# Gathering an expert's rows two turns ahead in a fused attention and mixture-of-experts kernel

## The chip, the cores and the metric

One Trainium2 chip, one of its cores. The metric is the device time of one launch in microseconds, lower is better; the number compared is the median of several runs. TensorE is written PE (its weight loads PEld), VectorE DVE, ScalarE ACT, GpSimd POOL, SyncE SP.

## What is computed

A linear attention block without a mask, then a mixture of experts in which each token goes to one expert or to none. Everything is float32. Cut to what matters:

```python
# q, k, v: (8, 8, 576, 64);  w1: (8, 512, 1024);  w2: (8, 1024, 512)
kv  = einsum('bhsd,bhse->bhde', k, v)
o   = einsum('bhsd,bhde->bhse', q, kv)
o   = o / sqrt(mean(o * o, -1) + 1e-6) * g_norm
x   = o.transpose(0, 2, 1, 3).reshape(4608, 512)       # one row for each token
do  = x @ w_skip > 0                                   # the others keep x
e   = argmax(x @ w_gate, axis=1); gate = softmax(x @ w_gate)[e]
out = x.copy()
for each expert i:                                     # over rows with do and e == i
    out[rows] = x[rows] + gate[rows] * (relu(x[rows] @ w1[i]) @ w2[i])
```

## The kernel before

The first third of the kernel is the attention. Its result x is written to the output tensor in HBM (`out_dram` in the profile), and from there on the output tensor is also the place from which the experts read their rows. While the last x is made, tokens are counted for each expert, experts are put in order of their token counts (largest first), and each token gets a slot number; the tables `src` (row to read for a slot) and `rows` (row to write) follow from that.

Then come eight turns, r = 0 to 7, one expert each (`experts`, L1276). Turn r holds between 256 and 352 slots, cut into pieces: two of 128 rows and, in turns 0 to 5, one or two smaller ones (64 or 32 rows, whose tables are `asrc` and `arows`). For each turn these steps are made:

- **Gather.** `gather_all` (L1269) takes a buffer `xg` from a pool that has three of them in rotation (`bufs=3`, L1271; turn 0 has a buffer of its own, `xg0`) and issues one indirect DMA from POOL for each piece (`gather_piece`, L1000 in the profile), which reads rows of `out_dram`.
- **Transpose.** `expert_in` (L1004, transposes at L1010, copies at L1013 and L1015) turns each piece on PE by a product with the identity and lets ACT copy it from PSUM into `xt`.
- **Layer 1.** `fast_1` (L1126) multiplies w1 and `xt` in a seven-product (Strassen) scheme; the products are in `product` (L1113), the sums they need are on DVE (L1055, L1061, L1117) and the copies on ACT (L1123). The relu writes `ht` (L1175, L1179). Turn 0 uses the plain `layer_1` (L1034).
- **Layer 2.** `fast_2` (L1186) does the same with `ht` and w2 for the first two pieces; the smaller ones are done plainly (`layer_2`, L1045).
- **Result.** `result` (L1246) multiplies by the gate, adds x in place in `xg` on DVE (L1252), and POOL issues an indirect DMA that scatters the rows to `out_dram` (L1255).

The order of instructions on each engine is the program's order: the block from L138 to L1395 is scheduled by hand, and a framework adds the waits. Three of its waits matter here, and all stand in the instruction lists:

- A gather reads `out_dram`, so it waits until all scatters issued before it have landed, and a scatter waits until all gathers issued before it have landed. Scatters do not wait for each other (L1259).
- `xg` of turn r + 3 is the buffer of `xg` of turn r, so a gather into it also waits for the transposes and the scatters of the earlier tenant.
- POOL's own queue is in order: gathers, scatters and the `blank` memset of the unused columns of `ht` (L1028) run one after another, and an instruction that waits holds those behind it.

In turn r the transposes are those of the **next** turn, r + 1: the first piece's are put into the end of `fast_1` (`between`, ahead of the last w1 product), the others directly after it (L1305, L1306), so that PE has `xt` for the next turn while layer 2 runs. Weights are loaded by SP (`load_weights`, L319 and L324), two turns' sets alternating between two pools.

Of the kernel before, what the change touches and what calls it, by code (L numbers as in the profile page):

```python
# [17 lines left out]
def kernel(  # L18
# [204 lines left out]
    for a in range(2):  # L223
        r = slice(a * 64, (a + 1) * 64)
# [679 lines left out]
    with tc.tile_pool(name="wpool_b", bufs=1, reuse_waits="tile") as wpool_b, \  # L904
# [92 lines left out]
        def gather_piece(xg, piece, src, asrc):  # L997
            off, m, col = piece
            idx = src if m == P else asrc
            nc.gpsimd.indirect_dma_start(  # L1000
                out=x_of(xg, off, m), out_offset=None, in_=cut_rows(m)[:, :],
                in_offset=bass.IndirectOffsetOnAxis(ap=idx[:, col:col + 1], axis=0))

        def expert_in(xg, xt, piece):  # L1004
            off, m, _ = piece
            x = x_of(xg, off, m)
            n = DC * m // P
            xp = bank()[:, :].rearrange("p (j t) -> p j t", t=P)
            for j in range(n):
                last = nc.tensor.transpose(out=xp[:, j, :], in_=x[:, j * P:(j + 1) * P],  # L1010
                                           identity=ident[:, :])
            if m == P:
                nc.scalar.copy(out=xt[:, :, off:off + P], in_=xp[:, :, :])  # L1013
            else:
                nc.scalar.copy(  # L1015
                    out=xt[:, :, off:off + m].rearrange("p (q j) t -> p q j t", j=n),
                    in_=xp[:, 0:n, :].rearrange("p j (q t) -> p q j t", t=m))
            return last

        def new_xt():  # L1020
            return ffn.tile([P, DC, CAP], FP32, tag="xt", name="xt")
# [8 lines left out]
        def layer_1(r, xt, ht, cols, fs):  # L1030
            for f in fs:
                hps = bank()
                for dc in range(DC):
                    nc.tensor.matmul(out=hps[:, cols], lhsT=w_sb[r][0][:, dc, f * P:(f + 1) * P],  # L1034
                                     rhs=xt[:, dc, cols], start=(dc == 0), stop=(dc == DC - 1))
                nc.scalar.activation(out=ht[:, f, cols], in_=hps[:, cols], func=ACT.Relu)
# [32 lines left out]
        def w1_sums(r):  # L1069
            w1 = w_sb[r][0]  # L1070
            s = wsum_pool.tile([P, 3, HD, F // 2], FP32, tag="s1", name="s1")
            sums[r, "w1"] = s
            lo, hi = slice(0, F // 2), slice(F // 2, F)
            parts = [combine((s[:, 0, d, :], s[:, 1, d, :], w1[:, d, hi], s[:, 2, d, :]),
                             w1[:, d, lo], w1[:, HD + d, lo], w1[:, d, hi], w1[:, HD + d, hi])
                     for d in range(HD)]
            return [job for both in zip(*parts) for job in both]
# [13 lines left out]
        def x_sums(r, xt, n):  # L1091
            t = ffn.tile([P, 3, HD, CAP // 2], FP32, tag="xs", name="xs", bufs=1)
            sums[r, "x"] = t
            lo, hi, a, b = slice(0, n), slice(n, 2 * n), slice(0, HD), slice(HD, DC)
            return list(combine_moving((t[:, 0, :, lo], t[:, 1, :, lo], xt[:, a, hi], t[:, 2, :, lo]),
                                       xt[:, a, lo], xt[:, a, hi], xt[:, b, lo], xt[:, b, hi]))
# [8 lines left out]
        def do(work, n=None):  # L1105
            n = len(work) if n is None else min(n, len(work))
            for job in work[:n]:
                job()
            del work[:n]
# [136 lines left out]
        def result(piece, yps, xg, tables, group):  # L1246

            off, m, col = piece
            n = DM * m // P
            rows, gate = tables[0 if m == P else 1]  # L1250
            x = x_of(xg, off, m)
            nc.vector.scalar_tensor_tensor(  # L1252
                out=x, in0=yps[:, 0:n], scalar=gate[:, col:col + 1], in1=x,
                op0=ALU.mult, op1=ALU.add)
            ins = nc.gpsimd.indirect_dma_start(  # L1255
                out=cut_rows(m)[:, :],
                out_offset=bass.IndirectOffsetOnAxis(ap=rows[:, col:col + 1], axis=0),
                in_=x, in_offset=None, bounds_check=N * P // m - 1, oob_is_err=False)
            tc.declare_no_dep(ins.ins, group=group, reason="each row has one slot")  # L1259
            tc.add_to_no_dep_group(group, ins.ins)  # L1260

        def load_ahead(r, behind=None):
            for ahead in (r, r + 1):
                if ahead < E and ahead not in w_sb:
                    load_weights(ahead, wpool_b if ahead % 2 else wpool_a, behind)
# [3 lines left out]
        def gather_all(r, pieces, src, asrc):  # L1269
            if r < E:  # L1270
                xgs[r] = xg0 if r == 0 else gather_pool.tile([P, CK, DM], FP32, tag="xg", name="xg",  # L1271
                                                             bufs=3)
                for piece in pieces[r]:
                    gather_piece(xgs[r], piece, src, asrc)

        def experts(pieces, widths, srcs, xt, ht, yps0, tables, group):  # L1276

            for r in range(E):
                load_ahead(r)
                if yps0 is not None and r == E - 1:  # L1280
                    nc.gpsimd.drain()
                if r:
                    gather_all(r + 1, pieces, *srcs)
                todo = pieces[r]
                end = widths[r]
                new = {}

                def enter(some):
                    for piece in some:
                        expert_in(xgs[r + 1], new["xt"], piece)  # L1290

                more = pieces[r + 1] if r + 1 < E else []
                if more:
                    new["xt"] = new_xt()
                beside = []
                if r == 0:
                    if yps0 is not None:
                        tables = first_tables(lambda fs: layer_1(r, xt, ht, slice(P, end), fs), tables)
                        result((0, P, 0), yps0, xgs[0], tables, group)
                    else:  # L1300
                        layer_1(r, xt, ht, slice(0, end), range(FC))
                    do(w1_sums(r + 1))
                    enter(more)
                else:
                    fast_1(r, xt, ht, end // 2, w2_sums(r), lambda: enter(more[0:1]))  # L1305
                    enter(more[1:])  # L1306
                if more:
                    n = widths[r + 1] // 2
                    beside = x_sums(r + 1, new["xt"], n) + (w1_sums(r + 1) if r else [])
                if r == 0:  # L1310
                    for piece in todo:
                        result(piece, layer_2(r, ht, piece), xgs[r], tables, group)
                        do(beside, 4)
                    do(beside)
                else:
                    if yps0 is not None and r == 1:
                        rnd_i = rounds()
                    if yps0 is not None and r == E - 1:
                        n_rounds.append(nc.values_load(rnd_i[0:1, 0:1], min_val=1,
                                                       max_val=ROUNDS + 1))  # L1320
                    of = {piece[0:2]: piece for piece in todo}
                    fast_2(r, ht, todo[2:], beside,
                           lambda key, y: result(of[key], y, xgs[r], tables, group))
                del w_sb[r]
                if more:
                    xt, ht = new["xt"], new_ht()
                    if yps0 is not None:
                        blank(ht, r + 1)
# [52 lines left out]
        def first_tables(layer, tables):  # L1381

            gp = g_ps[:, GB:GB + 3 * NCOL]
            half = NT // 2
            for i, t in enumerate((0, half)):
                bv = columns(t, half, colid_i, gate_k, 3, slot_pool, half)
                layer(range(i * FC // 2, (i + 1) * FC // 2))
                place(gp, bv, t, half, t == 0, t == half)
            gate = slot_gates_of(gp)
            agate = slot_pool.tile([P, NRES], FP32, tag="agate", name="agate")  # L1390
            nc.vector.tensor_copy(out=agate[:, :], in_=again_of(gate))
            return (tables[0], gate), (tables[1], agate)
# [56 lines left out]
```

## Time and profile before

| | |
|---|---|
| median of 3 runs | 396.01 us (393.86, 396.01, 396.41) |
| profiled execution, device time | 393.16 us |
| its span, first to last instruction | 391.4 us |
| PE busy, weight loads busy | 363.3 us (93%), 314.0 us (80%) |
| DVE, ACT, POOL busy | 242.8, 143.4, 124.1 us |
| mean granted TensorE clock | 0.984 |
| DMA | 81.70 MB, 209 GB/s over the span |
| layer 1 of turn 1 begins on PE | at 170.2 us of the span |
| last product on PE ends, then last result and scatter | 382.8 us, 391.4 us |

All times inside the profile are microseconds from the start of the span of the one profiled execution. The device time is 1.8 us more than the span. "Busy" is the time in which an engine executed something; the idle time in brackets after a row of the timeline is the gap on that engine directly before the row, with what ended it. Products on PE overlap each other in its pipeline and their ends are modelled. A row with x4 or x8 joins that many instructions. A DMA row on POOL is the time in which POOL makes the descriptors; the transfer itself lands later, and "landing" is the time from the issue until the data are there.

### The profile page before, as it was taken

The numbers are of one execution on the slowest core, as the hardware profiler recorded it, in microseconds if no ns is written. First come the engines' busy times: TensorE is split into PE (matmuls) and PEld (weight loads), VectorE is DVE, ScalarE is ACT, GpSimd is POOL, SyncE is SP. The second block draws the span as 40 slices with busy tenths as digits, with TensorE's granted clock in tenths as the row PEclk, the third lists the DMA queues.
The fourth block names the chain that finished last, engine by engine and source line by source line (L and its number), as shares of the span: only waits on it lengthen the run. The fifth ranks groups of instructions, "written<-read, shape, count | busy, mean of one in ns | idle before, by whom it ended". The sixth has DMA issues, their size and how long they took to land.

```text
span 391.4 us, 9585 instructions
## 1 busy us (share of the span) xinstructions
PE 363.3 (93%) x3822; PEld 314.0 (80%) x3822; DVE 242.8 (62%) x615; ACT 143.4 (37%) x384; POOL 124.1 (32%) x194
## 2 busy tenths in 40 slices
PE   7779999999987989999999999999999999989991
PEld 4668798898876668589879979989989878979980
DVE  3244458667778752765846657767667757858711
ACT  2445676666773212124303512512411421421410
POOL 7024557655677360123013303303303203202002
PEclk8999999999999999999999999999999999999997
DMA  8999999985597269654607355565564563511001
GB/s 298 394 392 391 402 399 403 399 261 182 161 381 241 55 202 358 234 175 151 216 15 272 77 201 163 180 216 154 178 216 145 171 229 102 198 27 56 2 2 51
DMA packets 31672, 81.70 MB, mean 209 GB/s; under 512 B 2106, under 2 KB 2114, under 8 KB 31620
## 3 DMA queue, kind: packets, MB, share of 16 engines
q1 hardware_dynamic: 27824, 69.47, 50.8%
q0 software_dynamic: 3776, 11.53, 8.7%
q8 instruction: 32, 0.52, 0.6%
q14 instruction: 20, 0.16, 0.1%
q10 hardware_dynamic: 20, 0.02, 0.0%
HBM read 66.80 MB, written 14.48 MB: 208 GB/s over the span
## 4 chain that ended last, share of the span: by engine, by line
PE 66%; issue 12%; DMA 9%; POOL 5%; DVE 3%; ACT 2%; SPq 1%; POOLq 0%; DVEq 0%; ACTq 0%
PE bank L1113 33%; PE bank L1045 7%; PE o_ps L471 7%; DMA out_dram<-xg,rows 4%; PE sum_ps L355 4%; PE q_ps L435 4%; PE bank L1034 3%; PE g_ps L369 3%; DMA q<-in_q_dram 2%; POOL xb L542 2%; DMA xg<-out_dram,src 2%; PE bank L1010 2%; POOL out_dram L1255 1%; PE g_ps L387 1%; DMA xg<-out_dram,asrc 1%
## 5 line engine op out<-in xcount | busy, mean ns | idle before, releaser
L1123 ACT COPY p<-bank 128x128 f32<-128x128 f32 (+6 forms) x70 | 20.8, 297 | 105.3 <-PE bank L1113 91.2
L1113 PE MATMUL bank<-xt,w 128*128 128x128 f32 (+5 forms) x336 | 55.4, 288 | 0.0
L542 POOL TENSOR_TENSOR xb<-xl,g_b 128x512 f32<-128x512 f32 x36 | 43.7, 1216 | 35.5 <-DVE rs L507 33.7
L1113 PEld LDWEIGHTS bank<-xt,w 128*128 128x128 f32 x336 | 47.0, 190 | 1.9 <-DVE bank L1117 1.4
L1117 DVE TENSOR_TENSOR bank<-bank,p 128x128 f32<-128x128 f32 (+6 forms) x70 | 23.6, 337 | 39.7 <-PE bank L1113 38.9
L1255 POOL DMA_INDIRECT out_dram<-xg,rows x16 | 16.2, 1012 | 75.6 <-DVE xg L1252 74.1
L471 PE MATMUL o_ps<-kvd,qT 128*128 128x146 f32 x240 | 37.0, 296 | 1.8 <-ACT kvd L391 0.7
L1113 PE MATMUL bank<-xs,s 128*128 128x128 f32 (+5 forms) x224 | 36.7, 289 | 0.0
L1045 PE MATMUL bank<-w,ht 128*32 128x128 f32 (+2 forms) x448 | 36.6, 322 | 0.0
L493 DVE TENSOR_REDUCE rs<-sq 128x8 f32<-128x512 f32 x36 | 24.5, 682 | 17.2 <-ACT sq L485 17.1
L471 PEld LDWEIGHTS o_ps<-kvd,qT 128*128 128x128 f32 x240 | 32.5, 193 | 3.3 <-ACT kvd L391 1.5
L1255 POOL DMA_INDIRECT out_dram<-xg,arows x8 | 9.0, 1127 | 76.6 <-DVE xg L1252 76.3
L1000 POOL DMA_INDIRECT xg<-out_dram,src x15 | 16.8, 1123 | 49.8 <-DMA out_dram<-xg,rows 27.4
L1113 PEld LDWEIGHTS bank<-xs,s 128*128 128x128 f32 x224 | 31.1, 190 | 1.0 <-ACT p L1123 0.8
L1045 PEld LDWEIGHTS bank<-w,ht 128*32 128x32 f32 (+2 forms) x448 | 20.4, 121 | 13.6 <-issue 10.9
L355 PE MATMUL sum_ps<-v,k 64*64 64x64 f32 x1152 | 26.0, 231 | 2.4 <-issue 2.2
L512 DVE TENSOR_TENSOR xl<-o_ps,rs 128x584 f32<-128x584 f32 x33 | 25.3, 766 | 4.3 <-PE o_ps L471 0.5
L1113 PE MATMUL bank<-w,ht 128*128 128x256 f32 x112 | 27.2, 386 | 0.0
L1113 PE MATMUL bank<-t,ht 128*128 128x256 f32 x112 | 27.1, 385 | 0.0
L355 PEld LDWEIGHTS sum_ps<-v,k 64*64 64x64 f32 x1152 | 22.2, 142 | 6.1 <-issue 3.8
L1113 PE MATMUL bank<-t,hs 128*128 128x256 f32 x112 | 25.3, 379 | 0.0
L485 ACT ACTIVATE sq<-o_ps 128x512 f32<-128x512 f32 x33 | 19.7, 597 | 15.2 <-PE o_ps L471 14.5
(203 smaller groups left out, 665.2 us busy)
## 6 DMA issues: line engine op xcount, KB each, us to landing
w<-in_moe_w_dram SPq DMA_DIRECT2D x16, 2048.0 KB, 8.7
q<-in_q_dram SPq DMA_DIRECT2D x8, 1152.0 KB, 9.0
k<-in_k_dram SPq DMA_DIRECT2D x7, 1152.0 KB, 12.1
v<-in_v_dram SPq DMA_DIRECT2D x7, 1152.0 KB, 15.2
out_dram<-xb SPq DMA_DIRECT2D x29, 256.0 KB, 9.0
out_dram<-xb POOLq DMA_DIRECT2D x7, 256.0 KB, 6.6
k<-in_k_dram SPq DMA_DIRECT2D x2, 576.0 KB, 5.2
v<-in_v_dram SPq DMA_DIRECT2D x2, 576.0 KB, 6.2
```

Source lines behind the costliest of these rows:

```text
L355: nc.tensor.matmul(out=sum_ps[w * 64:(w + 1) * 64, a, u, :], lhsT=kt[r, 2 * u + w, c, :], rhs=vt[r, 2 * u + w, c, :], start=(c == 0), stop ...
L471: nc.tensor.matmul(out=ps[:, w, 0:2 * PK].rearrange("p (r k) -> p r k", r=2)[:, :, cols], lhsT=qT[:, w, a, :], rhs=kvds[b % KVD][:, u, w, ...
L485: nc.scalar.activation(out=sq[:, :, :, :], in_=heads(ps, G, G + 2 * D), func=ACT.Square)
L493: nc.vector.tensor_reduce(out=rs[:, :, :], in_=sq[:, :, :, :].rearrange("p x y (a d) -> p x (y a) d", a=2), axis=AX.X, op=ALU.add)
L512: nc.vector.tensor_tensor(out=xl[:, :, :, :].rearrange("p x y (a k) -> p x (y a) k", a=2), in0=ps[:, :, 0:2 * PK].rearrange("p x (h k) -> ...
L542: late.append((lambda: nc.gpsimd.tensor_tensor(out=xb[:, :, 4 * u * D:(4 * u + 4) * D].rearrange("p r (w x) -> p r w x", w=2), in0=xl[:, : ...
L1000: nc.gpsimd.indirect_dma_start(out=x_of(xg, off, m), out_offset=None, in_=cut_rows(m)[:, :], in_offset=bass.IndirectOffsetOnAxis(ap=idx[:, ...
L1045: nc.tensor.matmul(out=yps[q * m:(q + 1) * m, 0:n], lhsT=ht[:, f, off:off + m], rhs=w_sb[r][1][:, f, q * n:(q + 1) * n], start=(f == 0), s ...
L1113: nc.tensor.matmul(out=out, lhsT=lhsT(i), rhs=rhs(i), start=start and i == 0, stop=i == k - 1, skip_group_check=True)
L1117: nc.vector.tensor_tensor(out=to, in0=x, in1=y, op=ALU.add)
L1123: nc.scalar.copy(out=t, in_=x)
L1255: ins = nc.gpsimd.indirect_dma_start(out=cut_rows(m)[:, :], out_offset=bass.IndirectOffsetOnAxis(ap=rows[:, col:col + 1], axis=0), in_=x, ...
```

## The change

In turn r (from 1 on) the rows gathered at the start of the turn are those of turn r + 2, where they were those of turn r + 1. The rows of turns 0 and 1 are still gathered before the first turn. Those of turn 2, which no turn would gather any more, are gathered in turn 0, after the transposes for turn 1 and before the results of turn 0 other than its first piece. Turns 6 and 7 now gather nothing (`gather_all` does nothing from r = 8 on). The number of gathers, what each reads and the three buffers stay as they are.

```diff
                 if yps0 is not None and r == E - 1:
                     nc.gpsimd.drain()
                 if r:
-                    gather_all(r + 1, pieces, *srcs)
+                    gather_all(r + 2, pieces, *srcs)
                 todo = pieces[r]
...
                 if r == 0:
+                    gather_all(2, pieces, *srcs)
                     for piece in todo:
                         result(piece, layer_2(r, ht, piece), xgs[r], tables, group)
                         do(beside, 4)
```

On POOL, the only engine whose instruction order changes, this moves the three gathers of turn 2 (128, 128 and 64 rows) from behind the `blank` memset at the end of turn 0 to directly behind turn 0's first scatter, ahead of its other three scatters and of that memset. From there on each turn's gathers stand at the same place in the queue as before, for an expert one further on; what stood there in turn 6 is gone.

## The prediction

> **What bounds the kernel now.** I read the page's totals first, then the busy time by turn, then the waits of the weight loads, and last the timeline around the transposes. The totals say which engine to follow:
>
> ```profile
> PE 363.3 (93%) x3822; PEld 314.0 (80%) x3822; DVE 242.8 (62%) x615; ACT 143.4 (37%) x384; POOL 124.1 (32%) x194
> PEclk8999999999999999999999999999999999999997
> ```
>
> The change touches only the expert turns, so I cut the span at the turns' borders (turns 1 to 6; columns: stretch, its length, busy time and instructions of PE, PEld, DVE, ACT, POOL, then granted clock, DMA share, GB/s):
>
> ```profile
> 170.00:206.00 36.00, 36.00 (x283) 31.00 (x272) 23.17 (x60) 9.77 (x26) 6.50 (x8) 1.00 0.43 144
> 206.00:240.00 34.00, 34.00 (x218) 29.93 (x218) 21.62 (x51) 9.43 (x26) 7.22 (x8) 1.00 0.50 167
> 240.00:268.00 28.00, 27.94 (x237) 25.05 (x236) 20.27 (x50) 8.79 (x26) 5.90 (x7) 1.00 0.56 186
> 268.00:298.00 30.00, 29.76 (x243) 26.61 (x242) 21.05 (x51) 8.91 (x26) 6.47 (x7) 1.00 0.56 179
> 298.00:329.00 31.00, 29.59 (x243) 26.45 (x242) 21.17 (x51) 8.55 (x25) 5.59 (x6) 1.00 0.52 172
> 329.00:357.00 28.00, 26.33 (x177) 24.24 (x176) 20.48 (x49) 8.46 (x25) 4.11 (x4) 1.00 0.35 113
> ```
>
> PE is busy for all of turns 1 and 2, and it falls behind the stretch in turns 5 and 6 by 1.4 and 1.7 us. DVE never exceeds 73% (20.48 of 28). So PE sets the pace, and where it idles, the span grows. The waits of PEld from 170 us on name the place, L1010, the transposes of the next turn's rows (us in total, times, longest):
>
> ```profile
> PEld bank L1010 <- PE bank L1113: 2.8, 4, 1.1
> PEld bank L1010 <- issue: 1.2, 1, 1.2
> PEld bank L1010 <- PE bank L1010: 0.6, 2, 0.3
> ```
>
> The releasers named there are not the true ones: a wait is put down to what ended last, and the PE instruction named is merely the one before. The DMAs show it. In turns 4 and 5 gathers on POOL (L1000) read so:
>
> ```profile
> 278.04 1.00 POOL L1000 DMA_INDIRECT xg<-out_dram,src  x1 [7.01 <-DMA out_dram<-xg,rows]
> ...
> 309.05 1.20 POOL L1000 DMA_INDIRECT xg<-out_dram,src  x1 [7.96 <-DMA out_dram<-xg,rows]
> 310.55 0.97 POOL L1000 DMA_INDIRECT xg<-out_dram,src  x1 [0.30 <-issue]
> ```
>
> and the transposes of turn 5 on PE, in the same turn,
>
> ```profile
> 312.73 0.63 PE L1010 MATMUL bank<-ident,xg 128*128 128x128 f32 x4 [0.97 <-DMA xg<-out_dram,src]
> 313.19 0.63 PE L1113 MATMUL bank<-xs,w 128*128 128x136 f32 x4
> 314.25 0.63 PE L1010 MATMUL bank<-ident,xg 128*128 128x128 f32 x4 [0.43 <-DMA xg<-out_dram,src]
> ```
>
> Issue at 309.05, transposes at 312.73; issue at 310.55, transposes at 314.25: each follows its own gather by 3.7 us, the median landing of these gathers being 3.6. The first of them had itself waited 8.0 us for the scatters of turn 4, issued until 300.9. So a turn's first layer (12 us in turn 5) has to cover a scatter's landing (8.3), 1.5 us of descriptors, and a gather's landing (3.6); as turns get shorter, it no longer does. In turns 1 and 2 the layers are 15 to 16 us long, and no wait stands before L1010.
>
> **The change, part by part.**
>
> *Removed: the waits at L1010.* After the change the rows transposed in turn r were asked for in turn r - 1, some 30 us earlier; a landing of 3.6 us, or even 7.9 (the longest), is over long before. In PEld's timeline the gaps before L1010 are 0.26 (turn 3, the small piece), 0.31 and 0.32 (turn 4), 1.14 and 0.60 (turn 5), 1.22 and 0.76 (turn 6): 4.61 us. PE's own rows give 0.97 + 0.43 + 1.05 + 0.60 = 3.05, since ends of products are modelled into the gap. To choose, I take starts, which are not modelled: from the start of the eight products ahead of the transposes to the first product of layer 2 it is 345.16 - 340.63 = 4.53 in turn 6, and 370.43 - 368.66 = 1.77 in turn 7, which has equal products (128 columns) and no transposes. Eight transposes at 0.11 (0.44 for four) add 0.88, so turn 6 should take 2.65 and loses 1.88; turn 7's 1.77 holds a gap of 0.15 that the transposes would cover, which makes the loss up to 2.03. PEld's 1.98 lies between, PE's 1.65 below. I take 4.6, with 3.1 as the least and 4.9 as the most (4.6 and 0.15 for each of the two turns whose gap may be covered).
>
> The Trainium skill, Perfetto Trace Analysis, section "Identifying the Most-Contended Engine", holds that matmul busy time misleads because pipelined products look smaller in the trace, and that weight-load time is the better measure. By that rule the gain is 4.6, by the matmul rows 3.1: 391.4 against 392.9.
>
> *Where the stall goes.* Next in line behind L1010 are layer 2's first product, which needs `ht` from ACT, and the DVE sums. Turns 1 and 2 are the pattern of a turn without the wait: there PE runs on into layer 2 with only 0.2 us of DVE's sum (L1117) before the transposes, which all turns have. Nearest row of a return: the 0.15 in turn 7. Bounds 0 and 4 x 0.15 = 0.6; I take 0, as turns 1 and 2 are the nearer rows. Weights do not come next: w1 for turn 6 is asked for at 283.05 and its first sum is made in turn 5's second layer, after 314, 30 us for a load whose median landing is 8.7.
>
> *Moved: the three gathers of turn 2 into turn 0.* On POOL they now stand behind the scatter of 157.82 and must see it land. The scatters' landings run from 2.4 to 8.6 us, so the gathers start between 160.2 and 166.4; three descriptors take 3 x (1.0 + 0.3) = 3.9, and the last lands 2.9 to 7.9 us after its issue, by 166 to 177. Behind them are turn 0's other three scatters (now at 165.85 to 171.95) and the memset of `ht` (171.94). They wait for that landing: three at 1.3 us, so the memset falls between 172 (when the last result is made) and 181. Who waits for them? The memset is needed by turn 1's 32-row products (L1045 at 200.92), 20 us or more off. The gathers themselves are needed by turn 1's transposes at 186.36: now they are issued at 178.39, in the changed kernel they are there by 177. The last scatter then lands by 189, turn 3's gathers are there by 200, and are needed at 221.75. Turn 1's first scatter, ready at 199.88, may wait a microsecond for them, which holds nothing but POOL. Cost 0, and no gain, since turn 1 has no wait at L1010 now: bounds 0 and 0. Without the cover of those 9 us before 186.36, each further microsecond of a late gather would be one of the span.
>
> Whether the descriptors are slowed beside DVE's sums in turn 0: the gather at 179.70, beside such sums, took 1.47 us for a usual 1.00. Three such would be 1.4 us more, inside the same cover.
>
> The Trainium skill, SBUF — State Buffer, section "SBUF: two separate sides", speaks against moving POOL's DMAs beside DVE: a GpSimd DMA that takes about 620 ns alone took about 3100 ns beside a DVE copy, since its descriptors could not be written. An estimate by that page is 2.5 us more for each of the three gathers, 7.4 in all, which would still be inside the 9 us; by the trace's 0.47 it is 1.4.
>
> *From turn 1 on* the gathers stand where they stood, released by the same scatters, into a buffer whose last scatters are the ones already waited for. Bytes and instructions are the same. Turn 6 loses its gathers from the queue, where nothing waited behind them but scatters due 16 us later. Cost 0. The tail after PE's last product, 8.6 us, stays.
>
> *Sum.* 393.16 of the profiled execution less 4.6 is 388.6. That execution is 2.85 below the median of the runs shown (396.01); a median run with the same waits gives 396.01 - 4.6 = **391.4**, or 1.2% less. About 1% is what a measurement of this kernel can tell from no change, so this lies close to that border.
>
> **The rivals.**
>
> *Smaller.* Only the 3.1 of PE's rows comes back, and up to 0.6 is returned at layer 2: 392.9 to 393.5. For it: PE's 29.59 of 31.00 and 26.33 of 28.00. Against it: the starts above. Chance 0.13.
>
> *Larger.* A run at the median has 2.85 us more than the profiled one, and if they lie in later landings (each microsecond of landing in turns 4 to 6 is paid twice a turn at most), the gain is up to 4.6 + 2.85 = 7.4: 388.6. Nothing in the profile shows where the slower runs lose; chance 0.10.
>
> *Hidden anyway.* The rows come early, yet the turn's length is set by something level with PE, or the gathers still wait for the scatter next before their use: 396.0. Against it: PE fully busy in turns 1 and 2, DVE at 73% at most, and the instruction lists, in which turn r's transposes wait for no DMA later than turn r - 1's gathers. Chance 0.06.
>
> *Slower.* One mechanism, in turn 0: the gathers of turn 2 stand behind the first scatter, and if they are late for 186.36, PE stops in turn 1 for the difference. That begins when that scatter takes over 17 us (157.8 + 17 + 3.9 + 7.9 = 186.6) and costs more than is won beyond 22 us. With 30 us, twice the longest landing of any write to `out_dram` (15.0), the last gather lands at 157.8 + 30 + 3.9 + 7.9 = 199.6, 12.2 after the second piece is due (187.4): 396.0 - 4.6 + 12.2 = 403.6. For it: a scatter beside a 2 MB weight load takes 8.3 us rather than 2.4. Against it: that is a quarter of what is needed, and the DMA engines are nearly idle (share 0.01) from 163 to 167. Chance 0.06.
>
> **How the numbers follow.** The forecast, 391.4, has 0.65; its own range is 390.5 to 392.9 (gains of 3.1 to 4.9, and 0.6 lower for a median that falls nearer the profiled execution). The range given runs from 388.6, the larger gain, to 394.5, which takes in the smaller one and a further microsecond of spread: 0.65 + 0.10 + 0.13 less their edges, somewhat over 8 in 10. Faster by over 1% means below 392.05: four fifths of the forecast (0.50) and the larger gain, 0.60. Within 1%: the rest of the forecast (0.15), the smaller and the hidden case, 0.34. Slower by over 1%: 0.06.
>
> **What would show it.** Right: no gap of PE or PEld before L1010 in turns 3 to 6, PE busy for all of these stretches, and the same 8.3 us scatter landings now followed only by POOL. On POOL in turn 0 the order is one scatter, three gathers at about 164 to 170, three scatters, with the memset at 171 to 181; the last result 4.6 us earlier. Wrong: gaps that stay at L1010, a gap at L1113 or L1045 in the next place, a transposition in turn 1 that waits for its gather, or a granted clock below 1.00 in the turns.

## The result and the profile after

The changed kernel took 388.85 us in the median of four runs (388.3 to 390.12) against 395.09 for the kernel before in four (393.86 to 396.41): a ratio of 0.985, 95% interval 0.980 to 0.990. Its profiled execution took 388.56, with a span of 386.8 where the kernel before had 391.4: 4.6 us less in the one pair of profiles, 6.2 in the medians. Why these two differ is a question of its own, taken up below. (In the run after_third below, two of twelve executions, 394.44 and 394.99 us, lay over 1.5% above its fastest and are left out of its median and ratio.)

The busy time in turns 5 and 6, of the changed kernel (columns as in the prediction: stretch, length, PE, PEld, DVE, ACT, POOL with their instructions, granted clock, DMA share, GB/s):

```profile
298.00:329.00 31.00, 30.99 (x259) 28.08 (x259) 22.80 (x55) 9.61 (x29) 6.86 (x8) 1.00 0.58 189
329.00:357.00 28.00, 27.98 (x196) 26.19 (x195) 22.41 (x55) 9.14 (x28) 1.97 (x2) 1.00 0.24 88
```

PE now fills the stretches that held 29.59 of 31 and 26.33 of 28. The waits of the changed kernel's weight loads from 170 us on are these, all of them:

```profile
PEld bank L1045 <- issue: 4.0, 12, 0.3
PEld bank L1113 <- issue: 3.5, 14, 0.4
PEld bank L1113 <- DVE bank L1117: 1.4, 7, 0.2
PEld bank L1113 <- ACT p L1123: 0.8, 5, 0.2
```

No row of L1010 is left. The first two rows were 4.0 and 3.5 before, and the 1.4 and 0.8 are also what they were: nothing has come in its place. PE around turn 6's transposes, in the timeline of the kernel before,

```profile
340.63 1.34 PE L1113 MATMUL bank<-xt,w 128*128 128x128 f32 x8
343.02 0.63 PE L1010 MATMUL bank<-ident,xg 128*128 128x128 f32 x4 [1.05 <-DMA xg<-out_dram,src]
343.49 0.61 PE L1113 MATMUL bank<-xs,w 128*128 128x128 f32 x4
344.69 0.63 PE L1010 MATMUL bank<-ident,xg 128*128 128x128 f32 x4 [0.60 <-DMA xg<-out_dram,src]
345.16 1.89 PE L1113 MATMUL bank<-w,ht 128*128 128x256 f32 x8
```

and in that of the changed kernel:

```profile
337.75 1.34 PE L1113 MATMUL bank<-xt,w 128*128 128x128 f32 x8
338.93 0.60 PE L1010 MATMUL bank<-ident,xg 128*128 128x128 f32 x4
339.36 0.61 PE L1113 MATMUL bank<-xs,w 128*128 128x128 f32 x4
339.81 0.60 PE L1010 MATMUL bank<-ident,xg 128*128 128x128 f32 x4
340.25 1.89 PE L1113 MATMUL bank<-w,ht 128*128 128x256 f32 x8
```

From the first start to the last it is 4.53 us before and 2.50 after. And POOL in turn 0, where the order was changed:

```profile
157.70 1.22 POOL L1255 DMA_INDIRECT out_dram<-xg,rows  x1 [12.49 <-DVE xg L1252]
164.74 0.98 POOL L1000 DMA_INDIRECT xg<-out_dram,src  x1 [5.83 <-DMA out_dram<-xg,rows]
166.03 1.22 POOL L1000 DMA_INDIRECT xg<-out_dram,src  x1 [0.30 <-issue]
167.55 0.94 POOL L1000 DMA_INDIRECT xg<-out_dram,asrc  x1 [0.30 <-issue]
171.44 1.02 POOL L1255 DMA_INDIRECT out_dram<-xg,rows  x1 [2.95 <-DMA xg<-out_dram,asrc]
172.77 1.26 POOL L1255 DMA_INDIRECT out_dram<-xg,arows  x1 [0.30 <-DVE t L1061]
174.34 0.98 POOL L1255 DMA_INDIRECT out_dram<-xg,arows  x1 [0.30 <-DVE bank L1117]
175.31 0.18 POOL L1028 MEMSET ht<- 128x64 f32 x1
```

POOL sits idle for 5.83 us before the gathers, which wait for the first scatter, and for 2.95 before the next scatter, which waits for the gathers. So the gathered rows are there by 171.44, 14.8 us before PE transposes the first of them at 186.24.

For everything below I use one measure that needs only starts: from PE's first product of turn 1 to the start of its last product. I call it the turns' time. It is 380.87 - 170.20 = 210.67 before and 375.96 - 170.07 = 205.89 after.

### The profile page after: what moved, and what is told of

It is laid out like the page before. It is cut to its first block, busy times and chain, and to the rows that moved or that the text cites. A ratio compares the mean times of both kernels' runs of the same rounds, so it can differ in the third digit from the quotient of the medians.

```text
span 386.8 us, 9583 instructions
## 1 busy us (share of the span) xinstructions
PE 361.9 (94%) x3822; PEld 314.0 (81%) x3822; DVE 242.8 (63%) x615; ACT 143.3 (37%) x384; POOL 124.0 (32%) x194
## 4 chain that ended last, share of the span: by engine, by line
PE 76%; issue 7%; DMA 6%; POOL 5%; DVE 3%; ACT 2%; POOLq 0%; SPq 0%; DVEq 0%; ACTq 0%
PE bank L1113 43%; PE bank L1045 8%; PE o_ps L471 7%; PE sum_ps L355 4%; DMA v<-in_v_dram 4%; PE q_ps L435 3%; PE bank L1034 3%; PE g_ps L369 2%; POOL xb L542 2%; PE bank L1010 2%; DMA k<-in_k_dram 1%; DMA xg<-out_dram,asrc 1%; PE g_ps L387 1%; POOL lp L529 1%; PE o_ps L454 1%
## 5 line engine op out<-in xcount | busy, mean ns | idle before, releaser
L1045 PE MATMUL bank<-w,ht 128*32 128x128 f32 (+2 forms) x448 | 36.6, 322 | 0.0
L1045 PEld LDWEIGHTS bank<-w,ht 128*32 128x32 f32 (+2 forms) x448 | 20.4, 121 | 13.6 <-issue 10.9
```

Of the source, the lines that this page charges most:

```text
L1045: nc.tensor.matmul(out=yps[q * m:(q + 1) * m, 0:n], lhsT=ht[:, f, off:off + m], rhs=w_sb[r][1][:, f, q * n:(q + 1) * n], start=(f == 0), s ...
```

## The experiments

The theory (A): a gather had to wait for the last turn's scatters to land, and one turn was too short for both landings; two turns ahead take that wait off PE, and nothing else changes. The main rival (B) after the first comparison: the gain is 6 us rather than 4.6, because ordinary executions wait longer at the transposes than the profiled one.

**The changed kernel again (after_again), no edit.**

> The changed kernel, timed anew against the kernel before. Theory A: the whole gain is the waits that the weight loads show at the transposes (L1010) in turns 3 to 6 of the kernel before, 0.26 + 0.63 + 1.74 + 1.98 = 4.6 us, so the ratio of the times is 0.988 (0.986 to 0.990), and the span of a profile 386.8. Rival B: the first comparison's 6.2 us (395.09 to 388.85) is the real size, because ordinary runs of the kernel before wait longer at L1010 than its profiled execution; then the ratio is 0.984.

Measured: median 389.42 (388.38 to 393.38) against 394.03 (392.82 to 397.16, 19 runs), ratio 0.989 (0.984 to 0.994): 4.6 us, as A says, not 6.2, though B's 0.984 lies at the very edge of the interval. Yet its profile fell on a long execution, with a span of 390.7. The turns' time in it is 205.88, as short as in the first profile; what was longer lies before turn 1, which began at 174.12 and not at 170.07. The granted clock (last column but two) fell there:

```profile
118.00:120.00 2.00, 1.33 (x36) 1.04 (x36) 1.83 (x5) 1.10 (x4) 1.84 (x5) 1.00 1.02 410
120.00:122.00 2.00, 0.34 (x1) 0.37 (x2) 1.73 (x5) 0.63 (x2) 1.84 (x6) 0.75 0.84 248
122.00:124.00 2.00, 2.00 (x11) 2.00 (x11) 1.75 (x2) 0.25 (x1) 2.00 (x4) 0.50 0.54 164
124.00:126.00 2.00, 2.00 (x11) 2.00 (x11) 1.11 (x5) 0.30 (x2) 0.56 (x3) 0.50 0.85 188
126.00:128.00 2.00, 2.00 (x12) 2.00 (x11) 1.59 (x3) 0.28 (x1) 1.46 (x1) 0.54 0.35 74
128.00:130.00 2.00, 2.00 (x30) 2.00 (x30) 0.00 (x0) 0.56 (x2) 1.93 (x3) 1.00 0.00 0
```

Between the attention and the experts PE idles in several places. In this execution the clock then fell to one half for some 6 us, and the first expert's first 40 products (L1034) took 7.65 us rather than 4.80. Between 144 and 150 it fell a second time, and 32 products of L1034 took 7.69 us rather than 6.00. The two profiles of the first comparison show 1.00 throughout this stretch.

**Gathers that wait for no scatter (other_source).** The kernel before, its later gathers reading the input q:

```diff
-        def gather_piece(xg, piece, src, asrc):
+        def q_rows(m):
+            x = q.rearrange("b h (s r) d -> (b h s) (r d)", r=8)
+            return x.rearrange("n (q d) -> (n q) d", q=P // m) if m < P else x
+
+        def gather_piece(xg, piece, src, asrc, rows_of=cut_rows):
...
-                out=x_of(xg, off, m), out_offset=None, in_=cut_rows(m)[:, :],
+                out=x_of(xg, off, m), out_offset=None, in_=rows_of(m)[:, :],
...
-                    gather_piece(xgs[r], piece, src, asrc)
+                    gather_piece(xgs[r], piece, src, asrc, q_rows if r > 1 else cut_rows)
```

> The kernel before, its gathers still one turn ahead, but from turn 2's rows on they read the same number of rows from the input q (viewed as 4608 x 512) in place of the output tensor, so that they no longer wait for the last turn's scatters to land; the experts then work on other rows than the reference's. Theory A (a gather was late because it waited 6 to 8 us for scatters): the gathers of turns 3 to 6 start 6 to 8 us earlier, no gap is left at L1010, and the time is that of the changed kernel, span 386.8 (386.3 to 387.3). Rival C (one turn is too short for descriptors and landing themselves, 1.3 + 3.6 us, or the transposes are held by something else): gaps of turns 5 and 6 stay at 1 us or more and the span is 389 or above.

Measured: span 386.4, turns' time 205.92, no wait of PEld at the transposes; median 389.94, ratio 0.990 (0.987 to 0.993). On POOL in turn 5 (every line number is 4 higher in this kernel, L1259 the scatter, L1004 the gather):

```profile
298.46 0.99 POOL L1259 DMA_INDIRECT out_dram<-xg,rows  x1 [0.30 <-PE bank L1117]
299.44 0.23 POOL L1032 MEMSET ht<- 128x128 f32 x1
299.84 1.52 POOL L1004 DMA_INDIRECT xg<-in_q_dram,src  x1 [0.17 <-issue]
301.66 0.97 POOL L1004 DMA_INDIRECT xg<-in_q_dram,src  x1 [0.30 <-issue]
```

From the last scatter to the next gather it is 1.4 us, where the kernel before has 9.2 (299.88 to 309.05). With the wait for the scatters gone, one turn ahead is enough, to 0.03 us. That settles what made the gathers late, and rules out descriptors and landing alone (rival C): these gathers even took 6.4 to 8.5 us to land (medians by turn, two 128-row pieces), where those of the kernel before took 3.5 to 4.0. The edit also frees the scatters from waiting for gathers; in the timeline of POOL each turn's first scatter waits for DVE's L1252 before and after (L1256 here), so that wait was not what was won.

**Turn 0's part undone (both_in_turn_1).**

```diff
-                if r:
+                if r == 1:
+                    gather_all(2, pieces, *srcs)
+                if r:
                     gather_all(r + 2, pieces, *srcs)
...
                 if r == 0:
-                    gather_all(2, pieces, *srcs)
```

> The changed kernel with the turn 0 part undone: the rows of turn 2 are gathered at the start of turn 1, as before, and those of turn 3 directly after them; from turn 2 on two turns ahead. Theory A: the move into turn 0 neither costs nor gains, so span 386.8 and the same time as the changed kernel within 0.3 us; turn 1 shows no gap at L1010. Rival D: three gathers ahead of turn 0's scatters cost or gain something (contention with weight loads, or an early transposition), then the difference is above 0.5 us.

Measured: turns' time 205.87, median 389.14 (after_again, beside it, 389.42), ratio 0.990 (0.984 to 0.995). The span is 387.6 and not 386.8: its turn 1 began 1.0 us later, after a fall of the clock like the one above. Turn 0's own second layer takes the same time too: from its first product (L1045) to turn 1 it is 12.45 us before (157.75 to 170.20), in the changed kernel (157.62 to 170.07) and here (158.63 to 171.08). The move into turn 0 is worth nothing and costs nothing; the line that the diff adds there could stand in turn 1 as well.

**Only turns 5 and 6 (from_turn_4), from the kernel before.**

```diff
-                if r:
+                if 1 <= r <= 4:
                     gather_all(r + 1, pieces, *srcs)
+                if r >= 4:
+                    gather_all(r + 2, pieces, *srcs)
```

> One turn ahead as in the kernel before up to turn 4, which gathers both turn 5's and turn 6's rows; from there on two turns ahead. Theory A: only the waits of turns 5 and 6 go, 1.74 + 1.98 = 3.7 us; gaps of about 0.3 stay in turn 3 and 0.6 in turn 4, and the span is 387.7 (387.4 to 388.1), about 0.9 us above the changed kernel. Rival E (the waits of turns 3 and 4 are given back later, so they are worth nothing): the same span as the changed kernel, 386.8.

Measured: turns' time 206.76, which is 0.87 above the changed kernel where 0.9 was expected, with 0.65 of it in two gaps before L1010 in turn 4; the weight loads show no gap in turn 3, where 0.3 was expected, but starts make that turn 0.15 longer. The span is 388.5, outside the expected 387.4 to 388.1, as its turn 1 began 1.1 us later than the changed kernel's, after a fall of the clock. Median 390.54, ratio 0.992 (0.989 to 0.995). Each wait is paid by itself and none is given back (rival E).

**A late gather in turn 0 (delay_13 and delay_26).** Memsets of a scratch tile on POOL:

```diff
                 if r == 0:
+                    if yps0 is not None:
+                        idle = slot_pool.tile([P, 1024], FP32, tag="idle", name="idle")
+                        for _ in range(13):                     # 26 in the second kernel
+                            nc.gpsimd.memset(idle[:, :], 0.0)
                     gather_all(2, pieces, *srcs)
```

> The changed kernel with 13 memsets of a scratch tile (128 x 1024, some 0.95 us each, 13 us together) on POOL in turn 0 between the first scatter and the gathers of turn 2. The prediction's cover: the gathers then start at about 172 in place of 164.7 and have landed by 179, ahead of turn 1's transposes at 186.2. Expected: no gap at L1010 in turn 1, and from turn 1's first product to the start of the last product the same 205.9 us as in the changed kernel. Rival (there is no such cover, a late gather is paid at once): 7 us more.

> The same with 26 memsets, some 26 us: the gathers start at about 185 and land at 188.6 to 191. Expected by the cover: transposes of turn 1 wait 2.4 us at the first piece and about 1 us at the others, so that turn 1 to the last product takes 209.3 us (208.3 to 210.3), 3.4 more than the changed kernel, though the gathers start 20 us later; later turns show no gap. Rival (no cover): some 20 us more. Rival (two turns ahead absorbs any lateness): 205.9.

Measured, one execution of each: with 13 the gathers start at 173.55 and turns' time is 205.88. The cover is there, though less of it is left than expected: the rows were expected by 179, and the scatter that waits for them goes at 183.04. With 26 they start at 186.20, and turns' time is 210.12, 4.2 more where 3.4 was expected (208.3 to 210.3 was the range). PE in turn 1 of the second kernel:

```profile
189.77 1.09 PE L1010 MATMUL bank<-ident,xg 128*128 128x128 f32 x4 [2.43 <-DMA xg<-out_dram,src]
190.65 1.35 PE L1113 MATMUL bank<-xs,w 128*128 128x172 f32 x4
191.80 1.46 PE L1010 MATMUL bank<-ident,xg 128*128 128x128 f32 x6
```

The first wait is the expected one (2.43 by PE's row, 2.66 by PEld's). The second, of about 1 us, is not there; in its place the four products between take 1.35 rather than 0.75, and the clock is 0.50 from 190 to 192. So the mechanism of the slower rival exists: a gather that is late enough stops PE. Where that begins lies between starts at 173.55 and 186.20; the prediction's 17 us, a start at about 175, was not tried by itself. It is the only profile in which the clock fell within the turns. Beside the waits of 1.1 us in the kernel before, it stayed at 1.00 (308 to 316).

**Two buffers before the change (two_buffers).**

```diff
-                                                             bufs=3)
+                                                             bufs=2)
```

> The kernel before with two buffers for the gathered rows in place of three. Theory A: one turn ahead uses two buffers only, the gather waits for the last turn's scatters anyway; from turn 1's first product to the start of the last product 210.7 us as before (210.2 to 211.2), the same gaps at L1010. Rival (the third buffer was in use, the pool's room mattered): gaps grow and the stretch is 212 or more.

Measured, one execution: turns' time 210.03, a little under the expected range, the waits in the same places. So the kernel before had no use for the third buffer. The changed one holds three turns' rows at once, by the order of its program; it was not run with two. The one time, 397.33, is long for another reason: its turn 1 began at 176.47. Of these 6.3 us, 2.6 had been lost before the first expert's first product (124.22 against 121.60), and after it the clock stood at 0.50 from 124 to 130 and at 0.70 from 145 to 150.

**Products that keep PE busy before turn 1 (warm),** on the changed kernel:

```diff
+    def warm(n):
+        for _ in range(n):
+            nc.tensor.matmul(out=g_ps[:, 0:2 * P], lhsT=ones[:, :],
+                             rhs=ones[:, :].unsqueeze(1).to_broadcast([P, 2, P]), start=True,
+                             stop=True, skip_group_check=True)
...
+        warm({NU - 3: 4, NU - 2: 3, NU - 1: 8}.get(n, 0))
         if n < NU:
             values(n)
...
+        warm(14)
         layer_1(0, xt_first, ht0, slice(0, P), range(0, 5))
...
         for piece in plan[0]:
+            warm(6 if piece is plan[0][-1] else 0)
             landed = expert_in(xg0, xt0, piece)
```

> The changed kernel with 35 small products on PE whose results nobody reads (ones by ones, 256 columns, some 0.11 us each) in the places where PE otherwise waits between the attention and turn 1: 4, 3 and 8 ahead of the last three attention units, 14 ahead of the first expert's first products (L1034), 6 ahead of turn 0's last transposed piece. In the runs so far the granted clock there fell to 0.50 for 5 to 8 us in four of six profiles. If the idle gaps bring that on: no fall below 1.00 between 110 and 150, a narrower spread of times, and a median some 1 us below the changed kernel, 388.2 (387.5 to 389). If they don't, or the products delay what follows: the same median or up to 1 us more.

Measured: 388.59 (387.33 to 389.74), ratio 0.987 (0.984 to 0.991); its clock in the stretch shown above:

```profile
120.00:122.00 2.00, 1.57 (x15) 1.29 (x12) 1.73 (x5) 0.30 (x1) 1.84 (x5) 1.00 0.82 193
122.00:124.00 2.00, 2.00 (x19) 1.98 (x19) 1.17 (x1) 0.56 (x2) 1.84 (x5) 1.00 0.55 121
124.00:126.00 2.00, 2.00 (x21) 2.00 (x21) 1.66 (x7) 0.63 (x3) 0.18 (x2) 1.00 0.87 227
```

Then both gather orders with these products, and the changed kernel without them, on one chip. before_warm has the edits of warm on the kernel before:

> The kernel before with the 35 idle-filling products, so that both gather orders can be compared without the falls of the granted clock ahead of turn 1. Theory A: before_warm less warm_again is the waits at L1010 alone, 4.6 us (4.0 to 5.0), in medians as in profiles; from turn 1's first product to the start of the last one 210.7 (210.0 to 211.2). Rival B: ordinary executions wait longer than profiled ones, then the medians differ by 6 or more.

> The changed kernel with the 35 products, again, beside the changed kernel without them on the same chip: median 388.6, 0.3 to 0.8 below it, and a spread of 2.5 us or less. If the falls of the clock are not what the spread comes from: no difference in median and the same spread of some 4 us.

> The changed kernel once more, on the same chip as the two others: median 389.2 (388.6 to 389.8), single times between 388 and 393.

Measured: after_third 389.85 in the median of ten times (388.45 to 391.96), ratio 0.990 (0.988 to 0.992); warm_again 388.15 (387.98 to 388.64), ratio 0.985 (0.982 to 0.987); before_warm 390.9 (389.27 to 392.82), ratio 0.991 (0.988 to 0.994). after_third came out just above its 389.8, and warm_again lies 1.7 us below it, where 0.3 to 0.8 was expected. With the products the changed kernel's times spread over 0.7 us here and 2.4 in warm, against 3.5 in after_third, and they make the best version that was run. That fits falls of the clock as a source of the spread, but they are not all of it: before_warm, with the same products and a clock of 1.00 in its profile from 104 to 176, spreads over 3.6 us, as much as the kernel before on that chip (392.42 to 395.99). In a kernel that gathers one turn ahead, the waits at the transposes vary too, as shown below.

For before_warm the expectation missed. Its turns' time is 208.95 and not 210.7, and 390.9 - 388.15 is 2.75, neither A's 4.6 nor B's 6. The profiles agree with the medians: warm_again's turns' time is 206.14, 2.81 less than before_warm's. So this pair gives no sign that ordinary executions lose more at the transposes than profiled ones do (rival B), but the size of the gain is not fixed. I looked at the kernel before once more, unchanged:

> The kernel before, unchanged, for one more profile of its waits. The stretch from turn 1's first product to the start of the last one was 210.7, 210.0 and 208.95 us in three profiles with one turn ahead, against 205.9 in all with two. If the wait varies from one execution to the next with the landing of the scatters: a value between 208.5 and 211, and the gaps before L1010 follow the time from the last scatter of a turn to the next gather. If the idle-filling products had shortened it: 210.5 or more here.

Measured: turns' time 210.64, which lies in the range of both answers and by itself decides nothing. By turns there is some of each. The wait varies between executions: against the changed kernel, by starts, turn 3 loses 0.23 us before, 0.72 in before_again, 0.14 with two buffers and 0.89 in before_warm. In turns 5 and 6 it is shorter with the products: 0.53 and 0.88 in before_warm, 1.10 to 1.84 and 1.63 to 2.15 in the three profiles without them. There the scatters land sooner: from the last scatter to the next gather it takes 9.17 and 8.89 us before, 9.15 and 9.03 in before_again, and 8.08 and 8.16 in before_warm. The DMA view of the stretch with turn 4's last scatters shows a difference; first the kernel before (297 to 309), then before_warm (296.5 to 308.5), GB/s in 40 slices and the row of queue q8, where there is one:

```profile
GB/s 0 0 0 14 177 157 123 41 184 300 273 328 321 375 362 416 355 382 355 205 184 150 157 294 437 457 348 416 403 396 396 362 219 123 27 27 20 27 7 0
...
q8 instruction: 1, 0.02, 0.5%
```

```profile
GB/s 0 0 0 0 0 130 143 191 48 96 341 300 218 246 328 396 375 416 362 341 294 239 164 102 259 416 410 403 403 410 437 437 376 328 150 7 0 0 0 0
```

In the kernel before a tail of some 27 GB/s follows the transfers for over a microsecond, and a 0.02 MB load of instructions (q8) lies in the stretch; before_warm has neither. The changed kernel has the tail and the q8 load in its turn 5, and warm has neither. The other profiles say the same. In the thirteen stretches of turns 5 and 6 without the products, of both gather orders, from the last scatter of a turn to the next gather, there is always such a load, and they last 8.68 to 9.32 us. In the four with the products there is none, and they last 8.08 to 8.16. The same step in turn 4 has no such load in any of the thirteen profiles in which gathers wait for scatters, with the products or without, and lasts 7.78 to 8.45. That the load of instructions holds up a part of the last scatter is argued from these stretches and was not tried by itself; why the products move the load is not known.

## Why the prediction was right, point by point

*The waits at L1010 are the whole change.* Shown, by other_source and from_turn_4. Counted from one turn's first product of layer 2 to the next turn's, the step to turn 3 became 0.23 us shorter, to turn 4 0.68, to turn 5 1.84 and to turn 6 2.03, against 0.26, 0.63, 1.74 and 1.98 in the prediction: 4.78 for 4.61. PE's own idle column (3.05) was the wrong one to add up, and the starts, with which the prediction chose, were the right check: 1.88 to 2.03 for turn 6. The Trainium skill's word in Perfetto Trace Analysis, "Identifying the Most-Contended Engine", that pipelined products mislead, holds here in this form: the rows of the products gave 3.05, those of the weight loads 4.61, and 4.78 was won.

*Nothing else becomes late.* Shown by the four rows of PEld's waits, which are the rows and sizes of before, and by from_turn_4, where each wait that stays is paid by itself.

*The moved gathers cost nothing.* Shown: both_in_turn_1 has the same turns' time. The first scatter landed 7.0 us after its issue (2.4 to 8.6 given), the memset came at 175.3 (172 to 181 given). The rows were there by 171.44 (166 to 177 given), so the cover was 14.8 us and not 9. The three descriptors took 0.98, 1.22 and 0.94 us; of the 2.5 us more for each that were estimated from SBUF — State Buffer, section "SBUF: two separate sides", these gathers beside DVE's sums show 0.2 at most. The copy of that estimate does not occur here: the rows of DVE beside them are sums of two tensors (L1061, 165.36 to 167.27) and the products with the gate (L1252). In all runs the longest row of a gather in the turns is 1.52 us.

*The rivals.* The smaller gain and the hidden one are out. The slower one's wait can be made (delay_26), but the changed kernel is 14.8 us away from it. The larger one is out as a price: its 7.4 us would be a ratio of 0.981, below the intervals of after_again (0.984 to 0.994) and after_third (0.988 to 0.992), and the latter leaves out B's 0.984 too. With the products medians and profiles give the same gain, 2.75 and 2.81. That the wait varies from one execution to the next, which it supposed, is so: 0.14 to 0.72 us in turn 3 and 1.10 to 1.84 in turn 5 without the products. after_again shows another place where a slow execution can lose, the falls of the clock before turn 1.

*The sum.* The span went from 391.4 to 386.8, the predicted 4.6; of the 4.78 in the turns and 0.13 gained before them, 0.3 was lost after PE's last product (from 10.5 to 10.8 us, counted from its start), which the prediction took as fixed. What was off is the base: 391.4 was made on a median of 396.01 out of three runs, while the later medians of the kernel before were 393.75 to 394.34. On 394.0 the same sum gives 389.4, and the changed kernel's medians were 388.85, 389.42 and 389.85. The step that failed is "a median run with the same waits gives 396.01 - 4.6": three runs that spread over 2.5 us were too few to set a level. That the first median, 388.85, still fell into the range is in part luck: the range reached down to 388.6 for the sake of the larger rival, whose gain was not what happened.

What the prediction did not foresee is that the gain depends on the landing. It is 4.78 us where the scatters of turns 4 and 5 take some 9 us to the next gather, and 2.8 between before_warm and warm_again, where they take 8.1. What stays open is why before_warm's scatters land earlier.

## What to carry to other kernels

When a buffer is filled from the tensor that the previous step writes to, count two landings, the write's and the read's, and ask a step earlier if the step is shorter than their sum; the third buffer may already be there. What is won is only what goes beyond the step's own length, so a microsecond more or less of landing changes it. Add up a stall from the starts of the instructions around it, on several profiles, and take a fixed stretch of the program as the measure, so that a change elsewhere in the run can't hide or fake the gain. A late request costs nothing until it meets its first use, so the place of such a request inside its slack needs no tuning.

## What the runs showed of the hardware

- The granted clock fell to 0.50 for some 4 to 8 us between 116 and 130 in nine of the eleven profiles without the filling products, after PE had idled for a few microseconds in pieces (busy 0.7 to 1.3 of each 2 us between 114 and 120 in most), in three of them a second time between 144 and 152, and once after a single wait of 2.4 us (delay_26). It stayed at 1.00 in the two profiles of the first comparison with the same idle pieces, so the idle time alone doesn't decide it. In the three profiles with 35 filling products it did not fall between 104 and 176, and their turn 1 began at 169.4 to 169.7, where it began at 170.1 and 170.2 in the two profiles without a fall, at 169.8 to 171.8 after one fall and at 174.1 or later after two.
- The two 128-row scatters of turns 4 and 5 beside a 2 MB load took 8.1 us, from the last issue to the next gather, in the kernels with the products and 8.7 to 9.3 in the others. As long as the rows were gathered one turn ahead, PE paid what that, the descriptors and the gather's landing came to beyond a turn's first layer: 1.10 us and more in turns 5 and 6 without the products, 0.53 and 0.88 with them.
